# Tile 0 of x loaded first, and three token tiles scaled on ScalarE, in the start-up of a Hedgehog linear-attention and MLP kernel

## The chip, the cores and the metric

The kernel runs on one core of a Trainium2 chip. Time is device time in microseconds (us), and smaller is better. Three runs of the kernel before took 687.21, 686.83 and 685.87 us, with a median of 686.83 us.

## The reference

With x of shape (2048, 640), 32 heads of 20 columns and a hidden width of 1536, the kernel must compute this:

```python
xn = layernorm(x)                               # per token, over 640 columns, eps 1e-5
q, k, v = split(xn @ wqkv)                      # 32 heads x 20
pq, pk = q @ w_phi[h], k @ w_phi[h]             # per head
phi_q = concat(softmax(pq), softmax(-pq))
phi_k = concat(softmax(pk), softmax(-pk))
kv, z = sum_s phi_k^T v, sum_s phi_k            # per head, over all 2048 tokens
s = (phi_q @ kv / (phi_q @ z + 1e-6)) @ wo
g = silu(gelu(xn @ w1 + b1) @ w2 + b2)
out = x + s * g
```

All arithmetic is float32. The kernel gets float32 precision out of TensorE's fp32r format by splitting each operand in a high part (a rounded copy) and a low part (the rest), and by adding three of the four cross products.

## The kernel before, in words

The 2048 tokens are 16 tiles of 128. Phase 1, which is where the change lies, first makes the folded key weights: for each of five chunks of 128 input rows, six TensorE products multiply a chunk of `wqk` (transposed, 384 KB per chunk) with a block diagonal of `w_phi` (`bd`, 360 KB), so that `xn @ wk` gives `pk` at once. `fold` (line 163) issues those products; `fold_w` copies the result out of PSUM as a high part on ScalarE (line 172) and a low part on VectorE (line 173). The folds of the query weights come later, spread over the loop.

A token tile goes through these steps. `x_in` (line 131) loads 128 rows of x. `stats` (lines 186 to 189) takes mean and variance on VectorE, adds eps there, and raises to the power -0.5 on GpSimd. `norm` (line 197) then subtracts the mean and multiplies by the reciprocal deviation over the whole tile, in place, on VectorE. `transpose_x` (line 292) transposes the tile on TensorE in five pieces; `plain` copies it out as a high part on ScalarE (line 226) and a low part on VectorE (line 228). For an odd tile this is in two pieces, `b` and `xp`. `project` (line 306) multiplies the tile with weights in 30 products. A projection has room in its middle, after three of its five chunks, for the transposes of the next tile.

`feat1` (lines 319 to 327) turns `pk` into exponents: maximum, minimum, difference on VectorE, and the negated half on GpSimd. `feat2` (line 332) is the exponential on ScalarE. The value weights `wv` are split in `split_w`: the high part on ScalarE (line 136), the low part on VectorE for chunks 0, 2 and 4 and on GpSimd for chunks 1 and 3 (both line 138). `value` (lines 349 to 354) is the projection with `wv`, and `kv_acc` (line 377) adds a tile's keys and values up. After phase 1 come the MLP and the output, on which TensorE works almost without a pause.

The order of the start-up is written by hand: `phase1` and `startup` are stretches in which each engine issues its instructions in the order of the program text, and an instruction that waits holds everything behind it on its engine. So the lines below are the queue of each engine, as far as each has a part in them. TensorE first runs eleven products of a matrix of ones with itself, whose result nobody reads (line 439).

PSUM has three double banks (`bankA`) for folds, transposes and projections. A step that takes a bank waits until the readers of the bank's last content are done. All loads of this stretch are issued by SyncE, on one queue, in the order of the text; a `stats` tile `st` has two buffers.

Of the kernel before, what the change touches and what calls it, by code (L numbers as in the profile page):

```python
# [8 lines left out]
F32 = mybir.dt.float32  # L9
F32R = mybir.dt.float32r  # L10
AF = mybir.ActivationFunctionType
OP = mybir.AluOpType
# [3 lines left out]
P = 128  # L16
# [29 lines left out]
def hedgehog_gated_mlp_kernel(ctx: ExitStack, tc: tile.TileContext, x, xt_in, wqk, bd, wv, wo, w1, b1, w2, b2, out_t):  # L46
    nc = tc.nc
# [3 lines left out]
    small = ctx.enter_context(tc.tile_pool(name="small", bufs=2))  # L51
# [25 lines left out]
    def slab(dt, name, shape=(P, 2, D)):  # L77
        return slabs.tile(list(shape), dt, tag="S", name=name)
# [4 lines left out]
    def bankA():  # L83
        return pools["A"].tile([P, 2, 512], F32, tag="A", name="pA")

    def bankB(name="pB"):
        return pools["B"].tile([P, 512], F32, tag="B", name=name)
# [41 lines left out]
    def load_x(t):  # L129
        xt = row([P, D], F32, "xt")  # L130
        nc.sync.dma_start(xt[:], x[_tok(t) * P:(_tok(t) + 1) * P, :])
        return xt
# [17 lines left out]
    def load_fold(which, mid=None):  # L150
        tl = folds[:, which]
        for c in range(KC):
            nc.sync.dma_start(tl[:, c], wqk[which, c, :, :6 * P].rearrange("p (i t) -> p i t", i=6))
            if c == 0 and mid is not None:
                mid()
        return tl

    def fold(tl, c):
        ps = bankA()
        for i in range(6):  # L160
            hf, j = divmod(i, 3)
            n = 120 if j < 2 else 80
            mm = nc.tensor.matmul(ps[:, hf, 120 * j:120 * j + n], tl[:n, c, i, :], foldb[:n, i, :n],  # L163
                                  start=True, stop=True)
        return ps, mm

    def fold_w(tl, cs, name, dst):
        for c in cs:
            ps, mm = fold(tl, c)
            sl = slab(F32R, f"{name}{c}")  # L170
            s3 = sl[:].rearrange("p s (a b) -> p s a b", a=2)
            nc.scalar.activation(s3[:, 0], ps[:, :, :HALF], AF.Copy)
            lo = nc.vector.tensor_tensor(s3[:, 1], ps[:, :, :HALF], s3[:, 0].bitcast(F32), op=OP.subtract)
            dst.append(sl)
        return mm, lo
# [5 lines left out]
    def stats(t, sm, mean, rstd):  # L181
        xt = xts.pop(t)
        st = sm[:, :12]
        for i in range(2):
            with tc.issue_after(last_feat[0].ins) if last_feat[0] is not None and not by_hand[0] else ExitStack():
                nc.vector.bn_stats(st[:, 6 * i:6 * i + 6], xt[:, i * HALF:(i + 1) * HALF])
        nc.vector.bn_aggr(sm[:, 12:14], st.rearrange("p (a b) -> p a b", a=2))
        nc.vector.tensor_scalar(rstd, sm[:, 13:14], LN_EPS, None, op0=OP.add)
        nc.gpsimd.tensor_tensor(rstd, rstd, mhalf[:], op=OP.pow)
        if mean is not None:  # L190
            nc.vector.tensor_copy(mean, sm[:, 12:13])
        return xt

    def norm(t):
        sm = small.tile([P, 16], F32, tag="st", name="st")
        xt = stats(t, sm, None, sm[:, 14:15])
        nc.vector.tensor_scalar(xt[:], xt[:], sm[:, 12:13], sm[:, 14:15], op0=OP.subtract, op1=OP.mult)
        xns[t] = xt

    W2 = 2 * P  # L200
# [85 lines left out]
    def transpose_x(t):  # L286
        q, o = divmod(t, 2)
        xn = xns.pop(t)
        ps = bankA()
        flat = ps[:].rearrange("p a b -> p (a b)")  # L290
        for k in range(KC):
            nc.tensor.transpose(flat[:, k * P:(k + 1) * P], xn[:, k * P:(k + 1) * P], ident[:])  # L292
        plain(q, o, flat[:, :D].rearrange("p (k t) -> p k t", t=P))
# [3 lines left out]
    def project(t, ws, mid=None):  # L297
        q, o = divmod(t, 2)
        ps = bankA()
        n = 0  # L300
        for k in range(KC):
            if k == 3 and mid is not None:
                mid()
            for a, b in PASSES:
                for hf in range(2):
                    nc.tensor.matmul(ps[:, hf, :HALF], stat_x(q, o, k, a),  # L306
                                     ws[k][:, b, hf * HALF:(hf + 1) * HALF],
                                     start=n == 0, stop=n == 3 * KC - 1)
                n += 1
        return ps  # L310
# [4 lines left out]
    def feat1(ps):  # L315
        p4 = heads(ps)
        mx = small.tile([P, 2, 16], F32, tag="mx", name="mx")
        mn = small.tile([P, 2, 16], F32, tag="mn", name="mn")
        nc.vector.tensor_reduce(mx[:], p4, axis=AX.X, op=OP.max)
        nc.vector.tensor_reduce(mn[:], p4, axis=AX.X, op=OP.min)  # L320
        e = slab(F32, "e")[:]
        e5 = e.rearrange("p a (h s d) -> p a h s d", s=2, d=DH)
        nc.vector.tensor_tensor(e5[:, :, :, 0, :], p4, mx[:, :, :, None].to_broadcast([P, 2, 16, DH]),
                                op=OP.subtract)
        nr = small.tile([P, 2, 16], F32, tag="nr", name="nr")
        last_feat[0] = nc.vector.tensor_tensor(nr[:], mn[:], mx[:], op=OP.subtract)  # L326
        nc.gpsimd.tensor_tensor(e5[:, :, :, 1, :], nr[:, :, :, None].to_broadcast([P, 2, 16, DH]),  # L327
                                e5[:, :, :, 0, :], op=OP.subtract)
        return e.rearrange("p a b -> p (a b)")
# [51 lines left out]
    vs, es, phis, xns, wk_s, wq_s = {}, {}, {}, {}, [], []  # L381
# [47 lines left out]
    def x_in(t):  # L429
        xts[t] = load_x(t)  # L430
# [4 lines left out]
    phase1 = ExitStack()  # L435
    phase1.enter_context(tc.manual_schedule(engines={mybir.EngineType.PE, mybir.EngineType.SP}))
    pw = bankA()
    for i in range(11):
        nc.tensor.matmul(pw[:, 0, :P], ones[:], ones[:], start=True, stop=True)
    startup = ExitStack()  # L440
    startup.enter_context(tc.manual_schedule())
    nc.sync.dma_start(foldb, bd)
    wkT = load_fold(1, lambda: x_in(0))
    x_in(1)
    x_in(2)
    wv_raw = [load_raw(wv[c * P:(c + 1) * P, :]) for c in range(KC)]
# [9 lines left out]
    def split_v(c):  # L456
        wv_s.append(split_w(wv_raw[c][:], "wv", "pool" if c % 2 else "dve"))

    norm(0)
    fold_w(wkT, range(2), "wk", wk_s)  # L460
    transpose_x(0)
    fold_w(wkT, range(2, 3), "wk", wk_s)
    norm(1)
    fold_w(wkT, range(3, KC), "wk", wk_s)
    kvp[0] = bankB("kv")
    pk = project(0, wk_s, lambda: transpose_x(1))
    norm(2)
    split_v(0)
    split_v(1)
    es[0] = feat1(pk)  # L470
# [5 lines left out]
    split_v(3)  # L476
    feat2(es[0])
    split_v(4)
    norm(3)
    es[1] = feat1(pk)  # L480
    vs[0] = value(0)
    phis[0] = key_fin(es.pop(0))
# [73 lines left out]
    t = NT - 1  # L556
# [494 lines left out]
```

## Time and profile before

| what | value |
|---|---|
| median of three runs | 686.83 us (685.87 to 687.21) |
| the profiled execution, its own time | 688.63 us |
| its span, from the first instruction of the program to the end of the last | 686.9 us |
| TensorE busy | 676.7 us (99%) |
| VectorE, GpSimd, ScalarE busy | 455.5, 375.6, 251.3 us |

The profiled execution took 1.73 us more than its span, and 1.80 us more than the median of the runs. Times in the views below count from the start of the span. In a timeline row stand the start, the length from the first to the last instruction of the row, the engine (PE is TensorE, PEld its weight loads, DVE is VectorE, ACT is ScalarE, POOL is GpSimd, SPq is SyncE's queue), the line, the operation, the tiles as output<-inputs, shapes, a count, and in brackets how long the engine stood idle before and what ended that. An fp32 product appears as two MATMUL records, so that the eleven products of ones are 22 and a fold of six products is 12. A row of the table by stretches gives for each engine its busy time and, in brackets, its instructions; then the granted TensorE clock, the share of the DMA engines that was busy, and GB/s.

### The profile page before, as it was taken

To read this page: it belongs to the slowest core of one execution; us is meant where nothing else is said; L and a number is where in the kernel's file an instruction comes from. 1 tells how busy PE (TensorE), PEld (TensorE's weight loads), DVE (VectorE), ACT (ScalarE), POOL (GpSimd) and SP (SyncE) were. 2 spreads that over 40 slices of the span, in tenths; PEclk is the share of its full clock that TensorE was granted. 3 is DMA by queue.
4 is the path that set the end of the run, shared out by engine and by line. 5 is a ranking of instruction groups with operands and counts; after the bars stand their busy time and mean duration, and the time that the engine had idled before them with its cause. 6 is when DMAs were issued, how large, how long until landed. Compare 5 with 4: busy or idle time off the path is not lost.

```text
span 686.9 us, 11941 instructions
## 1 busy us (share of the span) xinstructions
PE 676.7 (99%) x4713; PEld 590.6 (86%) x4713; DVE 455.5 (66%) x730; ACT 251.3 (37%) x398; POOL 375.6 (55%) x336
## 2 busy tenths in 40 slices
PE   8899999999999999999999999999999999999997
PEld 8899999999999998888887888888888887777875
DVE  4788566886876456677978774676977655774232
ACT  3332313323332237244353347633233354425430
POOL 1355244859577355866968853636456640783221
PEclk9999999999999999999999999999999999999999
DMA  9820052734261153329687697376364491886623
GB/s 339 305 88 2 3 150 81 242 79 149 51 216 59 80 171 134 115 70 329 211 301 260 210 421 319 90 266 240 140 206 153 145 396 49 314 295 210 231 93 107
DMA packets 73966, 125.73 MB, mean 183 GB/s; under 512 B 5694, under 2 KB 42558, under 8 KB 73014
## 3 DMA queue, kind: packets, MB, share of 16 engines
q1 hardware_dynamic: 71606, 114.48, 48.9%
q10 hardware_dynamic: 2304, 10.49, 4.2%
q8 instruction: 37, 0.61, 0.4%
q14 instruction: 19, 0.16, 0.1%
HBM read 79.85 MB, written 45.10 MB: 182 GB/s over the span
## 4 chain that ended last, share of the span: by engine, by line
PE 90%; DVE 5%; ACT 1%; issue 1%; DMA 1%; POOL 1%; SPq 0%; DVEq 0%; POOLq 0%; ACTq 0%
PE pA L306 30%; PE pB L645 22%; PE pB L616 18%; PE pB L804 11%; PE pB L746 3%; PE pB L735 2%; PE kv L377 2%; PE pA L163 2%; DVE y L654 2%; DVE xhi L670 1%; DMA xt<-in_x_dram 1%; PE pA L292 1%; PE pB L753 1%; DVE rc L340 0%; PE pB L590 0%
## 5 line engine op out<-in xcount | busy, mean ns | idle before, releaser
L645 PE MATMUL pB<-hs,w2s 128*128 128x512 f32 x720 | 167.1, 390 | 0.0
L645 PEld LDWEIGHTS pB<-hs,w2s 128*128 128x128 f32 x720 | 134.7, 188 | 29.2 <-PE pB L746 0.8
L616 PE MATMUL pB<-xp,w1s 128*128 128x512 f32 x324 | 81.4, 390 | 1.0 <-DVE pB L888 1.0
L616 PE MATMUL pB<-xd,w1s 128*128 128x512 f32 x324 | 79.3, 389 | 0.0
L332 ACT ACTIVATE e<-e 128x1280 f32<-128x1280 f32 x32 | 40.7, 1272 | 91.5 <-POOL e L327 91.0
L804 PE MATMUL pB<-oT,wo 128*128 128x512 f32 x300 | 72.9, 394 | 0.0
L616 PEld LDWEIGHTS pB<-xp,w1s 128*128 128x128 f32 x324 | 60.7, 188 | 13.9 <-DVE pB L888 1.4
L654 DVE TENSOR_TENSOR y<-pB,y 128x512 f32<-128x512 f32 x100 | 63.9, 680 | 12.3 <-PE pB L645 12.1
L616 PEld LDWEIGHTS pB<-xd,w1s 128*128 128x128 f32 x324 | 60.8, 188 | 12.6
L804 PEld LDWEIGHTS pB<-oT,wo 128*128 128x128 f32 x300 | 55.4, 188 | 14.8 <-ACT ph L738 1.2
L345 POOL TENSOR_TENSOR e<-e,rc 128x1280 f32<-128x1280 f32 x16 | 39.0, 2440 | 48.5 <-DVE rc L365 48.2
L345 POOL TENSOR_TENSOR eq<-eq,rc 128x1280 f32<-128x1280 f32 x16 | 38.0, 2372 | 50.0 <-DVE rc L704 50.0
L327 POOL TENSOR_TENSOR e<-nr,e 128x640 f32<-128x640 f32 x32 | 45.4, 1421 | 33.5 <-DVE nr L326 30.7
L306 PE MATMUL pA<-wv,xp 128*128 128x320 f32 x384 | 61.0, 312 | 0.8 <-DVE nr L326 0.4
L621 ACT ACTIVATE pB<-pB,b1t 128x512 f32<-128x512 f32 x48 | 31.8, 662 | 77.3 <-DVE pB L888 28.4
L306 PE MATMUL pA<-wk,xp 128*128 128x320 f32 x384 | 59.9, 311 | 0.0
L306 PE MATMUL pA<-wq,xp 128*128 128x320 f32 x384 | 59.0, 309 | 0.0
L306 PEld LDWEIGHTS pA<-wv,xp 128*128 128x128 f32 x384 | 56.9, 188 | 1.7 <-issue 0.7
L306 PEld LDWEIGHTS pA<-wq,xp 128*128 128x128 f32 x384 | 56.9, 188 | 0.1
L306 PEld LDWEIGHTS pA<-wk,xp 128*128 128x128 f32 x384 | 56.8, 188 | 0.1
L691 POOL TENSOR_TENSOR ez<-eq,zrep 128x1280 f32<-128x1280 f32 x16 | 47.3, 2953 | 1.1 <-PE pB L753 1.1
L401 POOL TENSOR_TENSOR w1s<-raw,w1s 128x640 fp32r<-128x640 f32 (+1 forms) x18 | 25.7, 1429 | 36.8 <-ACT w1s L400 29.6
(139 smaller groups left out, 1046.0 us busy)
## 6 DMA issues: line engine op xcount, KB each, us to landing
raw<-in_w_dram SPq DMA_DIRECT2D x42, 320.0 KB, 4.4
e_dram<-e ACTq DMA_DIRECT2D x16, 640.0 KB, 3.3
eq<-e_dram SPq DMA_DIRECT2D x16, 640.0 KB, 6.9
phi_dram<-eq SPq DMA_DIRECT2D x16, 640.0 KB, 3.4
phi<-phi_dram SPq DMA_DIRECT2D x16, 640.0 KB, 9.5
xt<-in_x_dram SPq DMA_DIRECT2D x16, 320.0 KB, 4.8
xres<-in_xt_dram SPq DMA_DIRECT2D x20, 256.0 KB, 4.5
out_dram<-xres SPq DMA_DIRECT2D x18, 256.0 KB, 3.0
```

The costliest lines, as they stand in the source:

```text
L306: nc.tensor.matmul(ps[:, hf, :HALF], stat_x(q, o, k, a), ws[k][:, b, hf * HALF:(hf + 1) * HALF], start=n == 0, stop=n == 3 * KC - 1)
L327: nc.gpsimd.tensor_tensor(e5[:, :, :, 1, :], nr[:, :, :, None].to_broadcast([P, 2, 16, DH]), e5[:, :, :, 0, :], op=OP.subtract)
L332: nc.scalar.activation(ef, ef, AF.Exp)
L345: nc.gpsimd.tensor_tensor(e3, e3, rc[:, :, None].to_broadcast([P, 64, DH]), op=OP.mult)
L401: nc.gpsimd.tensor_tensor(sl[:, 1, :n], src, sl[:, 0, :n].bitcast(F32), op=OP.subtract)
L616: nc.tensor.matmul(bank[ch][:], tl[:, a, off + wo_:off + wo_ + P], mov(blk, b), start=new and n == 0, stop=n == len(mms) - 1, skip_group_c ...
L621: nc.scalar.activation(ps, ps, AF.Gelu_apprx_tanh, bias=b1t[:, f:f + 1])
L645: nc.tensor.matmul(ps[:], ws[i][:, b, d * P:(d + 1) * P], hs[o][i][:, a, :], start=i == n == 0, stop=(i, n) == (GF - 1, 2), skip_group_che ...
L654: nc.vector.tensor_tensor(y, ps[:], y, op=OP.add)
L691: nc.gpsimd.tensor_tensor(zv, ef, zf, op=OP.mult)
L746: nc.tensor.matmul(po[64 * e:64 * e + 64, :256], bdk[:n, 2 * j + e, :], ph[:n, e * 256:(e + 1) * 256], start=True, stop=True)
L804: nc.tensor.matmul(ps[:], w, o, start=n == 0, stop=n == 15)
```

## The change

Three things are changed, all in the start-up. The load of tile 0 of x is issued ahead of `bd` and of the first chunk of `wqk`, where it stood third. TensorE runs fourteen products of ones instead of eleven. For tiles 1, 2 and 3, `norm` is replaced by two steps: `norm_stats` takes the statistics as before and then forms minus mean times reciprocal deviation, a 128x1 instruction on VectorE, and `norm_apply` computes x times scale plus bias over the tile on ScalarE. The statistics of tile 2 stand ahead of the first projection, where `norm(2)` stood behind it. Tile 0 and tiles 4 to 15 are treated as before.

```diff
+    def norm_stats(t):
+        sm = small.tile([P, 16], F32, tag="st", name="st")
+        xt = stats(t, sm, None, sm[:, 14:15])
+        nc.vector.tensor_scalar(sm[:, 15:16], sm[:, 12:13], sm[:, 14:15], -1.0, op0=OP.mult, op1=OP.mult)
+        nb[t] = xt, sm
+
+    def norm_apply(t):
+        xt, sm = nb.pop(t)
+        nc.scalar.activation(xt[:], xt[:], AF.Identity, bias=sm[:, 15:16], scale=sm[:, 14:15])
+        xns[t] = xt
...
-    for i in range(11):
+    for i in range(14):
         nc.tensor.matmul(pw[:, 0, :P], ones[:], ones[:], start=True, stop=True)
...
+    x_in(0)
     nc.sync.dma_start(foldb, bd)
-    wkT = load_fold(1, lambda: x_in(0))
+    wkT = load_fold(1)
     x_in(1)
     x_in(2)
...
     fold_w(wkT, range(2, 3), "wk", wk_s)
-    norm(1)
+    norm_stats(1)
     fold_w(wkT, range(3, KC), "wk", wk_s)
+    norm_apply(1)
+    norm_stats(2)
     kvp[0] = bankB("kv")
     pk = project(0, wk_s, lambda: transpose_x(1))
-    norm(2)
+    norm_apply(2)
     split_v(0)
     split_v(1)
     es[0] = feat1(pk)
...
     split_v(4)
-    norm(3)
+    norm_stats(3)
+    norm_apply(3)
     es[1] = feat1(pk)
     vs[0] = value(0)
```

The new lines move the numbering: what is line 172 and 173 stays, line 226 and 228 become 239 and 241, line 306 becomes 319, and so on by 13 (further down by up to 17). The order of each engine shows what the text does to the queues. VectorE, from the sum of tile 1's statistics to the low part of the transposed tile 1 (`b_272` or `b_283`, and `xp`), before:

```order
L187 BN_AGGR st<-st 128x2
L188 TENSOR_SCALAR st<-st 128x1
L197 TENSOR_SCALAR xt<-xt,st 128x640
L173 TENSOR_TENSOR wk_233<-pA,wk_233 128x640
L173 TENSOR_TENSOR wk_243<-pA,wk_243 128x640
L228 TENSOR_TENSOR b_272<-pA,b_272 128x2x128
L228 TENSOR_TENSOR xp<-pA,xp 128x3x128
L186 BN_STATS st<-xt 128x6 x2
L187 BN_AGGR st<-st 128x2
L188 TENSOR_SCALAR st<-st 128x1
L197 TENSOR_SCALAR xt<-xt,st 128x640
```

and the same place in the change:

```order
L187 BN_AGGR st<-st 128x2
L188 TENSOR_SCALAR st<-st 128x1
L205 TENSOR_SCALAR st<-st 128x1
L173 TENSOR_TENSOR wk_236<-pA,wk_236 128x640
L173 TENSOR_TENSOR wk_246<-pA,wk_246 128x640
L186 BN_STATS st<-xt 128x6 x2
L187 BN_AGGR st<-st 128x2
L188 TENSOR_SCALAR st<-st 128x1
L205 TENSOR_SCALAR st<-st 128x1
L241 TENSOR_TENSOR b_283<-pA,b_283 128x2x128
L241 TENSOR_TENSOR xp<-pA,xp 128x3x128
```

The two instructions over the whole tile (line 197) are gone from VectorE, two of one column (line 205) have come, and tile 2's statistics stand ahead of tile 1's low part instead of behind it.

ScalarE, from the high part of the last key weights to the first value copy `v`, in the change:

```order
L172 ACTIVATE wk_246<-pA 128x640
L210 ACTIVATE xt<-xt,st 128x640
L239 ACTIVATE b_283<-pA 128x2x128
L239 ACTIVATE xp<-pA 128x3x128
L210 ACTIVATE xt<-xt,st 128x640
L136 ACTIVATE wv<-raw 128x640 x3
L239 ACTIVATE xp<-pA 128x5x128
L136 ACTIVATE wv<-raw 128x640
L345 ACTIVATE e<-e 128x1280
L136 ACTIVATE wv<-raw 128x640
L210 ACTIVATE xt<-xt,st 128x640
L367 ACTIVATE v<-pA 128x32x20
```

Without its three rows of line 210 this is the order before. The row for tile 1 stands ahead of the high part of transposed tile 1 (`b_283`, `xp`), the one for tile 2 ahead of the five splits of `wv`, and the one for tile 3 behind them and ahead of `v`.

SyncE's first loads, in the change:

```order
L131 DMA xt<-in_x_dram 128x640
L456 DMA folds<-in_bd_dram 128x720
L153 DMA folds<-in_wqk_dram 128x768 x5
L131 DMA xt<-in_x_dram 128x640 x2
L144 DMA raw<-in_wv_dram 128x640 x5
```

Before, `bd` stood first, one load of `wqk` second, tile 0 of x third, and four loads of `wqk` behind it.

More of the change, by code (lines that the diff above doesn't have):

```diff
@@ L197, in norm @@
         nc.vector.tensor_scalar(xt[:], xt[:], sm[:, 12:13], sm[:, 14:15], op0=OP.subtract, op1=OP.mult)
+        xns[t] = xt
+    nb = {}
+    def norm_stats(t):
[6 more added lines that the diff above has]
+        nc.scalar.activation(xt[:], xt[:], AF.Identity, bias=sm[:, 15:16], scale=sm[:, 14:15])
         xns[t] = xt
```

## The prediction

> **What bounds the kernel now.** I read the busy shares first, then the table by stretches, then the timeline of the start. TensorE is the bound, and its idle time lies in the first 35 us:
>
> ```profile
> PE 676.7 (99%) x4713; PEld 590.6 (86%) x4713; DVE 455.5 (66%) x730; ACT 251.3 (37%) x398; POOL 375.6 (55%) x336
> ...
> 6.20:7.70 1.50, 1.46 (x13) 1.31 (x11) 0.07 (x1) 0.00 (x1) 0.00 (x0) 1.00 1.03 389
> ...
> 8.70:10.40 1.70, 1.53 (x13) 1.41 (x13) 0.98 (x4) 0.14 (x1) 0.56 (x1) 1.00 1.02 406
> ...
> 20.00:24.20 4.20, 2.94 (x21) 2.70 (x20) 3.40 (x7) 1.19 (x2) 2.07 (x2) 1.00 0.95 370
> ...
> 26.60:35.00 8.40, 7.61 (x49) 7.06 (x49) 5.24 (x12) 2.60 (x3) 3.87 (x3) 1.00 0.94 279
> 35.00:80.00 45.00, 45.00 (x552) 43.99 (x551) 35.92 (x66) 12.32 (x17) 21.52 (x25) 1.00 0.11 32
> 80.00:680.00 600.00, 599.02 (x3952) 516.00 (x3951) 397.43 (x624) 226.93 (x364) 344.85 (x284) 1.00 0.55 188
> ```
>
> From 35 to 80 us TensorE has no gap, and from 80 to 680 us it has 0.98 us. So what it gains before 35 us reaches the end, as long as the engines that feed it move ahead too. Behind 8.70 us the gaps are 0.17 (8.70 to 10.40), 1.26 (20 to 24.2) and 0.79 us (26.6 to 35): 2.22 us in all. The timeline names them:
>
> ```profile
> 1.20 5.07 PE L439 MATMUL pA<-ones 128*128 128x128 f32 x22 [1.20 <-POOL ones L102]
> 6.06 1.60 PE L163 MATMUL pA<-folds 120*128 120x120 f32 x12
> 8.66 1.56 PE L163 MATMUL pA<-folds 120*128 120x120 f32 x12 [0.99 <-DMA folds<-in_wqk_dram]
> 10.39 0.74 PE L292 MATMUL pA<-ident,xt 128*128 128x128 f32 x5 [0.17 <-DVE xt L197]
> 20.10 1.92 PE L306 MATMUL pA<-wk,b 128*128 128x320 f32 x12
> 24.16 0.74 PE L292 MATMUL pA<-ident,xt 128*128 128x128 f32 x5 [1.26 <-DVE xt L197]
> 27.09 3.17 PE L306 MATMUL pA<-wv,xp 128*128 128x320 f32 x20 [0.44 <-DVE nr L326]
> 30.50 2.11 PE L306 MATMUL pA<-wv,xp 128*128 128x320 f32 x10 [0.24 <-POOL wv L138]
> 35.09 0.71 PE L292 MATMUL pA<-ident,xt 128*128 128x128 f32 x5
> ```
>
> The first fold has its data when the products of ones end. The second waits 0.99 us for its chunk. The transposes of tile 0 wait 0.17 us and those of tile 2 1.26 us for the scaled tile, and the first value projection waits for its bank and then for `wv`.
>
> **Scaling and statistics.** What delays tile 2, and all that stands behind it on VectorE, is this:
>
> ```profile
> 16.62 1.55 DVE L173 TENSOR_TENSOR wk<-pA,wk 128x640 fp32r<-128x640 f32 x2
> 19.68 0.55 DVE L228 TENSOR_TENSOR xp<-pA,xp 128x384 fp32r<-128x384 f32 x1
> 20.14 0.88 DVE L186 BATCH_NORM_STATS2 st<-xt 128x6 f32<-128x320 f32 x2
> 21.30 0.16 DVE L188 TENSOR_SCALAR st<-st 128x1 f32<-128x1 f32 x1
> 22.19 1.83 DVE L197 TENSOR_SCALAR xt<-xt,st 128x640 f32<-128x640 f32 x1 [0.73 <-POOL st L189]
> 23.94 0.81 DVE L138 TENSOR_TENSOR wv<-raw,wv 128x640 fp32r<-128x640 f32 x1
> 26.87 0.18 DVE L326 TENSOR_TENSOR nr<-mn,mx 128x32 f32<-128x32 f32 x1
> 30.88 0.82 DVE L138 TENSOR_TENSOR wv<-raw,wv 128x640 fp32r<-128x640 f32 x1 [2.37 <-ACT wv L136]
> 33.66 0.61 DVE L197 TENSOR_SCALAR xt<-xt,st 128x640 f32<-128x640 f32 x1 [0.73 <-POOL st L189]
> ...
> 22.12 1.55 POOL L138 TENSOR_TENSOR wv<-raw,wv 128x640 fp32r<-128x640 f32 x1
> 27.13 1.79 POOL L327 TENSOR_TENSOR e<-nr,e 128x640 f32<-128x640 f32 x1 [3.46 <-DVE nr L326]
> ...
> 19.19 2.00 ACT L136 ACTIVATE wv<-raw 128x640 fp32r<-128x640 f32 x3
> 30.13 0.72 ACT L136 ACTIVATE wv<-raw 128x640 fp32r<-128x640 f32 x1
> 32.71 0.71 ACT L354 ACTIVATE v<-pA 128x640 f32<-128x640 f32 x1 [1.86 <-PE pA L306]
> ```
>
> Scaling a tile cost VectorE 0.61 us twice and 1.83 us for tile 2, where it ends with GpSimd's `wv` (22.12 + 1.55 = 23.67). The Trainium skill (SBUF — State Buffer, "Who interferes with whom") has a lock for this: such a VectorE instruction and GpSimd's share a port pair, and the second waits for the first. The trace agrees (23.67 plus a part of 0.61 is 24.02); by that rule ScalarE never waits so, and the sum stays the same with or without it.
>
> No row shows the new ScalarE scaling. The nearest, a 128x640 copy, took 0.72 us from SBUF; with a column as bias it may be longer, so I bound it by 0.71 (the copy out of PSUM in the last row) and twice that, and take 0.72 as it reads and writes just as much. The new 128x1 step is like L188, 0.15 us, which is also its lower bound; 0.61, the whole tile, is its upper.
>
> The new times, if TensorE ran as before: VectorE has the last low part of the key weights at about 17.7 instead of 18.17 (0.46 less scaling). Tile 2's statistics follow at once. From their start to the reciprocal deviation it took 22.15 - 20.14 = 2.0 us; with the new step, 19.9. ScalarE is through with tile 1's copies when it begins on `wv`, at 19.2, so tile 2 is scaled at 20.65 instead of 24.02. TensorE wants it at 24.16 - 1.26 = 22.9: **the 1.26 us go**, with 2.2 us to spare. The price is paid by tile 1's low part, which slips from 20.23 to about 20.9; its first half is out at 20.3 and TensorE, which starts on tile 1 at 20.10 with four products of the high part (0.16 us each), wants it at 20.7, so that is covered, by 0.4 us. (Were the step 0.61, half of that is gone.)
>
> ScalarE's splits of `wv` start at 20.65 instead of 19.19. VectorE's first one thus ends near 22.2 instead of 24.75, and `feat1` of tile 0, 2.3 us in the trace (24.75 to 27.05), near 24.5: **the bank wait of 0.44 us goes**. GpSimd's `e` (1.79) ends near 26.4 and its second `wv` (1.55 like the first) near 28.0. TensorE, rid of its gaps, reaches that chunk's low part at 30.50 - 0.24 - 1.70 = 28.6. From the end of `e` to that of the last low part, over the exponential and two splits, the rows give 31.70 - 28.92 = 2.8 us, so it is there near 29.2, when TensorE needs it near 29.7 (2.05 us before 31.7). So **the last 0.35 us go** as well, by margins of 0.5 us.
>
> New waits: line 210 for tile 3 stands ahead of `v`, whose bank the transposes of tile 3 take. From the end of the last `wv` low part (31.70) to the reciprocal deviation was 33.66 - 31.70 = 1.96 us; so the new step ends at 31.3, the scaling at 32.0 and `v` (0.71) at 32.75. TensorE was there at 35.09 and will be at 35.09 - 2.05 = 33.0: covered, by 0.3 us. `feat1` of tile 1 starts behind the new step instead of behind 0.61 us of scaling, near 31.3 instead of 34.27, so the keys of later tiles lead more than TensorE does.
>
> Sum behind the transposes of tile 0: 1.26 + 0.44 + 0.35 = **2.05 us saved**.
>
> **Order of loads and products of ones.** The first loads, in the order of the queue, and how long each took from issue to landing (for the second, third, fourth and sixth place):
>
> ```profile
> 1.25 0.42 SPq L153 DMA_DIRECT2D folds<-in_wqk_dram  x1
> 1.72 0.42 SPq L131 DMA_DIRECT2D xt<-in_x_dram  x1
> 2.19 1.85 SPq L153 DMA_DIRECT2D folds<-in_wqk_dram  x4
> ...
> folds<-in_wqk_dram SPq DMA_DIRECT2D x1, 384.0 KB, 3.4
> xt<-in_x_dram SPq DMA_DIRECT2D x1, 320.0 KB, 5.9
> folds<-in_wqk_dram SPq DMA_DIRECT2D x1, 384.0 KB, 6.4
> folds<-in_wqk_dram SPq DMA_DIRECT2D x1, 384.0 KB, 7.3
> ...
> 7.63 0.89 DVE L186 BATCH_NORM_STATS2 st<-xt 128x6 f32<-128x320 f32 x2 [5.78 <-DMA xt<-in_x_dram]
> 9.63 0.61 DVE L197 TENSOR_SCALAR xt<-xt,st 128x640 f32<-128x640 f32 x1 [0.68 <-POOL st L189]
> ```
>
> So the second, third and fourth place landed near 4.65, 7.6 and 8.6. Tile 0 goes from third place to first: landing to scaled is 10.24 - 7.6 = 2.6 us, so it is ready before 7.3 even if it lands like the second place. That removes the 0.17 us. But the first chunk of `wqk` goes from second to third, and through the third place the same 1,064 KB have to come. From the row it lands at 7.6, where the first fold started at 6.06. From the other side: if it comes as early as the second place did plus its own 384 KB at 389 GB/s (1.0 us), it is there at 5.7. I take 7.6, the same place in the queue. The fourth place does not change.
>
> The three products of ones are six records more: at the pace of the first 22 (4.86/22 = 0.221 us) 1.33 us, at that of the folds (1.60/12 = 0.133) 0.80 us. They end at 6.9 to 7.4, inside the wait for the chunk; without that cover they would cost their full 0.80 to 1.33 us.
>
> So the folds run 7.63 to 9.23 and on to 10.79, their 1.60 and 1.56 us back to back, and the transposes start at 10.79 instead of 10.39: **0.40 us lost**.
>
> **Sum.** -2.05 + 0.40 = -1.65 us, against the profiled execution's own 688.63: 686.98. The median of the runs shown is 1.80 us lower, so 686.83 - 1.65 = **685.2 us**.
>
> **Rivals.**
>
> - *The chunk lands early (5.7).* The folds then wait only for the fourth place at 8.6, end at 10.22, and tile 0 is ready: all 2.22 us are saved, 684.6. For it: the third place took 2.5 us more than the second for 320 KB more, which are 0.8 us at 389 GB/s; such a delay need not recur. Against it: the transfers moved 389 GB/s up to 7.7 us, so the queue was full.
> - *A new wait on ScalarE.* `v` and the last splits now stand behind scalings that wait for statistics, with margins of 0.3 to 0.5 us. If the scaling takes 1.4 us instead of 0.72, once ahead of the splits and once ahead of `v`, `v` ends at 32.75 + 1.36 = 34.1, the transposes of tile 3 start 1.1 us later and 0.55 us is left: 686.3. The same side has executions in which early loads come fast: there tile 0 was no wait before either, and the added products cost their 0.80 us: 2.05 - 0.80 = 1.25, 685.6.
> - *TensorE falls back to the slower pace (slower than before).* Its first 22 records ran at 0.221 us and the folds at 0.133, so TensorE has a slower pace, and products of ones lead out of it. If the chunk comes at 9.0 (7.3 us after issue, as long as the slowest `wqk` load took), TensorE stands idle some 2 us ahead of its folds, more than the 0.99 us that did no harm. The transposes then start at 12.2, 1.8 us late; if the slower pace returns for 4.86 us, 22 records lose 0.09 us each, 1.9 us. 1.8 + 1.9 - 2.05 = +1.65: 688.5. It is beyond 0.2% from a landing near 8.7 on, and only with the slower pace; the late landing alone ends at -0.25.
>
> *A page beside the last rival.* By the Trainium skill (TensorE: Matmul & The Clock Gate, "What's actually happening") the clock opens after a busy window of about 3.4 us and closes after an idle one of that length, free-running. The 4.86 us at the slower pace agree with it; by it 2 us of idleness would close nothing and the last rival would be -0.25 us, and more products of ones would open the clock no sooner.
>
> **How the numbers follow.** Chances: forecast 0.45 (its own range 684.8 to 685.8, as the chunk and the margins move it by a few tenths), early chunk 0.22, new wait or nothing to gain from loads 0.26, slower pace 0.07. A measurement of this kernel tells a change of 0.2%, 1.37 us, from none, so faster is below 685.46. The forecast is there in two of three cases (0.31), the early chunk always (0.22), the third hardly (0.03): 0.56 faster. Same has the rest of the forecast, of the third and a part of the last: 0.39. Slower: 0.05. The range goes from 684.1, all gaps closed and half a microsecond of the spread of the runs, to 686.8, the new wait with the same.
>
> **What would show it.** Right: the first chunk's fold starts behind a DMA wait near 7.6; tile 2's transposes, the first value projection and its `wv` have no idle time ahead of them; no transposes of tile 3 wait for ScalarE; TensorE is full from about 9 us on. Wrong: a wait of TensorE for line 210 or for `v`, fold records above 0.133 us, or gaps behind 35 us that give the lead back.

## The result and the profile after

The changed kernel took 684.45 us in the median of seven runs (683.99 to 686.25). Seven runs of the kernel before, the three shown among them, have a median of 686.70. The ratio is 0.9972, with a 95% interval from 0.9960 to 0.9983: 1.9 us saved (1.2 to 2.7), where 1.65 were forecast. The two medians lie 2.25 us apart, inside that interval.

The profiled execution took 684.19 us with a span of 682.4. That is 4.4 us less than the one of before, and more than the change is worth, as the second trace of each kernel shows further down.

The stretches of the changed kernel that answer to those shown of before (TensorE's busy time and records come first, GB/s last):

```profile
20.00:24.20 4.20, 4.20 (x32) 4.19 (x31) 3.60 (x6) 3.15 (x5) 1.97 (x2) 1.00 1.04 405
26.60:35.00 8.40, 8.06 (x54) 7.29 (x53) 6.44 (x12) 3.20 (x5) 2.51 (x6) 1.00 0.68 207
35.00:80.00 45.00, 45.00 (x553) 44.00 (x551) 33.86 (x65) 12.17 (x19) 20.75 (x25) 1.00 0.11 31
80.00:680.00 600.00, 597.63 (x3939) 514.52 (x3937) 397.44 (x622) 226.33 (x362) 345.47 (x281) 1.00 0.55 188
```

The 1.26 us between 20 and 24.2 us are gone. (In the last row TensorE's last product ends inside the stretch; up to there the trace shows no wait of TensorE behind 35 us.) The timeline of TensorE in the changed kernel, and then of its weight loads:

```profile
1.20 5.93 PE L452 MATMUL pA<-ones 128*128 128x128 f32 x28 [1.20 <-POOL ones L102]
6.96 2.80 PE L163 MATMUL pA<-folds 120*128 120x120 f32 x24
9.60 0.71 PE L305 MATMUL pA<-ident,xt 128*128 128x128 f32 x5
21.79 0.71 PE L305 MATMUL pA<-ident,xt 128*128 128x128 f32 x5
24.10 5.19 PE L319 MATMUL pA<-wv,xp 128*128 128x320 f32 x30
32.15 0.77 PE L305 MATMUL pA<-ident,xt 128*128 128x128 f32 x5 [0.22 <-ACT v L367]
...
27.18 0.88 PEld L319 LDWEIGHTS pA<-wv,xp 128*128 128x128 f32 x6 [0.25 <-POOL wv L138]
28.43 0.59 PEld L319 LDWEIGHTS pA<-wv,xp 128*128 128x128 f32 x4 [0.37 <-DVE wv L138]
32.15 0.53 PEld L305 LDWEIGHTS pA<-ident,xt 128*128 128x128 f32 x5 [0.48 <-ACT v L367]
```

The folds follow the products of ones without a wait, as their first chunk had landed 4.5 us after its issue at 1.73 us, and the transposes of tile 0 and tile 2 (rows at 9.60 and 21.79) have none either. The value projection at 24.10 starts at once, but inside it the weight loads wait 0.25 us for GpSimd's and 0.37 us for VectorE's low part of `wv`. The transposes of tile 3 wait for `v`, which they did not before.

VectorE, GpSimd's splits of `wv` and ScalarE in the changed kernel:

```profile
18.77 0.21 DVE L205 TENSOR_SCALAR st<-st 128x1 f32<-128x1 f32 x1 [0.73 <-POOL st L189]
20.60 0.83 DVE L138 TENSOR_TENSOR wv<-raw,wv 128x640 fp32r<-128x640 f32 x1 [0.82 <-ACT wv L136]
23.54 0.18 DVE L339 TENSOR_TENSOR nr<-mn,mx 128x32 f32<-128x32 f32 x1
27.55 0.82 DVE L138 TENSOR_TENSOR wv<-raw,wv 128x640 fp32r<-128x640 f32 x1 [2.36 <-ACT wv L136]
...
21.27 1.57 POOL L138 TENSOR_TENSOR wv<-raw,wv 128x640 fp32r<-128x640 f32 x1 [2.54 <-ACT wv L136]
25.55 1.58 POOL L138 TENSOR_TENSOR wv<-raw,wv 128x640 fp32r<-128x640 f32 x1
...
19.02 0.92 ACT L210 ACTIVATE xt<-xt,st 128x640 f32<-128x640 f32 x1 [0.67 <-DVE st L205]
19.84 1.98 ACT L136 ACTIVATE wv<-raw 128x640 fp32r<-128x640 f32 x3
30.58 0.93 ACT L210 ACTIVATE xt<-xt,st 128x640 f32<-128x640 f32 x1 [3.06 <-DVE st L205]
31.41 0.68 ACT L367 ACTIVATE v<-pA 128x640 f32<-128x640 f32 x1
```

ScalarE scales a tile in 0.92 us; tile 2 is ready at 19.94, where TensorE wants it at 21.79. The last two rows show the new wait: `v` had to stand behind the scaling of tile 3.

### The profile page after: what moved, and what is told of

Same layout as the page of the kernel before. It is cut to its first block, busy times and chain, and to the rows that moved or that the text cites. A ratio compares the mean times of both kernels' runs of the same rounds, so it can differ in the third digit from the quotient of the medians.

```text
span 682.4 us, 11960 instructions
## 1 busy us (share of the span) xinstructions
PE 676.1 (99%) x4719; PEld 591.2 (87%) x4719; DVE 452.7 (66%) x730; ACT 253.9 (37%) x401; POOL 376.9 (55%) x336
## 4 chain that ended last, share of the span: by engine, by line
PE 96%; DVE 1%; POOL 1%; ACT 1%; issue 1%; POOLq 0%; DVEq 0%
PE pA L319 29%; PE pB L662 24%; PE pB L633 22%; PE pB L821 11%; PE pB L763 3%; PE pB L752 2%; PE kv L390 2%; PE pA L163 2%; PE pA L452 1%; PE pA L305 1%; PE pB L770 1%; DVE st L186 0%; DVE wk L173 0%; PE pB L607 0%; ACT wv L136 0%
```

## The experiments

Eleven kernels were run, and of three of them a second execution was profiled. The chips differ, so the ratio compares each kernel with runs of the kernel before on the same chip, whose medians were 686.46 to 686.70 us. From the traces two numbers were read (starts of rows of the timeline, in us): when the transposes of tile 0 start, which is what loads and products of ones decide, and how long it is from there to the transposes of tile 3, which is what scaling and statistics decide, as long as TensorE runs at its full pace.

| kernel | loads | products of ones | tile 0 | tile 0 to tile 3 | median us | ratio (95%) |
|---|---|---|---|---|---|---|
| before, first trace | old | 11 | 10.39 | 24.70 | 686.70 | |
| before, second trace | old | 11 | 9.48 | 24.70 | | |
| load order alone | new | 11 | 10.06 | 24.53 | 686.88 | 1.0006 (0.9996 to 1.0016) |
| scaling and statistics alone | old | 11 | 9.17 | 22.51 | 684.61 | 0.9970 (0.9960 to 0.9980) |
| the change, first trace | new | 14 | 9.60 | 22.55 | 684.45 | 0.9972 (0.9960 to 0.9983) |
| the change, second trace | new | 14 | 10.09 | 22.56 | | |
| with 11 products | new | 11 | 12.47 | 23.29 | 685.14 | 0.9985 (0.9972 to 0.9998) |
| the same, second trace | new | 11 | 9.56 | 22.53 | | |
| with 6 products | new | 6 | 11.92 | 23.30 | 688.77 | 1.0030 (1.0020 to 1.0041) |
| `v` first | new | 14 | 9.49 | 22.15 | 684.64 | 0.9969 (0.9958 to 0.9980) |
| statistics of tile 2 late | new | 14 | 10.30 | 25.01 | 687.32 | 1.0007 (0.9999 to 1.0015) |
| scaled on VectorE | new | 14 | 9.21 | 23.63 | 686.43 | 0.9997 (0.9989 to 1.0005) |
| `wv` on VectorE | old | 11 | 9.46 | 21.53 | 683.38 | 0.9952 (0.9939 to 0.9965) |
| the same, new loads | new | 14 | 10.68 | 21.53 | 684.10 | 0.9962 (0.9948 to 0.9975) |

### The load order alone

```diff
+    x_in(0)
     nc.sync.dma_start(foldb, bd)
-    wkT = load_fold(1, lambda: x_in(0))
+    wkT = load_fold(1)
```

> The load order alone: tile 0 of x first, eleven products of ones, scaling and statistics as before. Theory (order and scaling are two separate gains): the transposes of tile 0 start near 9.6 us as in the changed kernel, 0.8 us sooner than in the trace of before, all later waits of before stay as they are (1.26 us ahead of the transposes of tile 2, about 0.8 us at the first value projection), so 0.4 to 0.8 us are saved: near 686.1. Rival (the early landing of the first chunk in the one trace was luck; the third place lands near 7.6 again): the transposes start near 10.8, 0.4 us are lost: near 687.1.

686.88 us, ratio 1.0006: nothing gained. TensorE now waits ahead of the first fold instead of the second:

```profile
1.20 4.50 PE L439 MATMUL pA<-ones 128*128 128x128 f32 x22 [1.20 <-POOL ones L102]
7.16 3.07 PE L163 MATMUL pA<-folds 120*128 120x120 f32 x24 [1.45 <-DMA folds<-in_wqk_dram]
10.06 0.71 PE L292 MATMUL pA<-ident,xt 128*128 128x128 f32 x5
23.66 0.73 PE L292 MATMUL pA<-ident,xt 128*128 128x128 f32 x5 [1.25 <-DVE xt L197]
```

The theory's 0.4 to 0.8 us are refuted; the rival's 687.1 is inside the interval. The later waits (1.25 us here) are those of before, as both had it.

### Scaling and statistics alone

The change with the load order and the eleven products of before.

```diff
-    x_in(0)
     nc.sync.dma_start(foldb, bd)
-    wkT = load_fold(1)
+    wkT = load_fold(1, lambda: x_in(0))
...
-    for i in range(14):
+    for i in range(11):
```

> Scaling on ScalarE and the earlier statistics alone: bd and the first chunk of wqk ahead of tile 0, eleven products of ones. Theory: the start up to the transposes of tile 0 is that of before, and behind it 1.26 us ahead of the transposes of tile 2, the bank wait of 0.44 us and part of the 0.35 us are gone: 1.8 to 2.1 us saved, near 684.7. Rival (the lead of the changed kernel comes from the loads): under 1 us saved, above 685.7, with a wait left ahead of the transposes of tile 2.

684.61 us, 0.9970: the whole gain of the change, as the theory had it. Loads and products of ones add nothing that can be measured.

### The change with eleven and with six products of ones

```diff
-    for i in range(14):
+    for i in range(11):
```

> The whole change with eleven products of ones instead of fourteen. Theory (the three products only fill the wait for the first chunk): the first fold starts when its chunk lands, near 6.3 us instead of 6.96, the second still waits for its own chunk near 7.7, so the transposes of tile 0 start 0 to 0.3 us sooner and the time is that of the changed kernel within 0.3 us: 684.1 to 684.5. Rival (without them TensorE falls back to its slower pace): fold records of 0.22 us instead of 0.13, 1 to 2 us lost, 685.5 or more.

685.14 us, and its twelve runs are spread from 684.15 to 688.42. The profiled one is the longest of them:

```profile
1.20 5.06 PE L452 MATMUL pA<-ones 128*128 128x128 f32 x22 [1.20 <-POOL ones L102]
7.30 5.38 PE L163 MATMUL pA<-folds 120*128 120x120 f32 x24 [1.04 <-DMA folds<-in_wqk_dram]
12.47 1.27 PE L305 MATMUL pA<-ident,xt 128*128 128x128 f32 x5
13.54 4.39 PE L163 MATMUL pA<-folds 120*128 120x120 f32 x36
```

Behind a wait of 1.04 us the 24 fold records took 5.38 us, 0.22 us each, where the change had 2.80. The median lies between the theory (684.1 to 684.5) and the rival (685.5 or more), but this execution has the rival's slow records. A longer wait did no harm with the load order alone (1.45 us), so a second execution was profiled.

> The whole change with eleven products of ones, looked at once more. Theory (the wait for the first chunk decides by chance whether TensorE keeps its slower pace): if the wait is 0.5 us or less, folds at 0.13 us a record and about 684.4; if it is 1 us as in the first trace, folds at 0.22 us until about 14 us and 686 to 688.4. Rival (the pace has nothing to do with the wait): the one without the other.

The one run took 685.24 us and shows this:

```profile
1.20 4.24 PE L452 MATMUL pA<-ones 128*128 128x128 f32 x22 [1.20 <-POOL ones L102]
6.74 2.99 PE L163 MATMUL pA<-folds 120*128 120x120 f32 x24 [1.29 <-DMA folds<-in_wqk_dram]
```

A longer wait, 1.29 us, and folds at full pace: the theory as written falls, since it had the length of the wait decide. What differs is the row ahead. Here the 22 records of ones took 4.24 us, so TensorE had come to its full pace before the wait; in the first trace they took 5.06, 0.23 each to the end, so it had not.

With six products this is forced, as they end long before that point:

```diff
-    for i in range(14):
+    for i in range(6):
```

> The whole change with six products of ones: they end near 3.9 us, and TensorE stands idle until the first chunk lands, 2.5 to 3.3 us. Theory (an idle stretch ahead of the folds keeps TensorE at its slower pace, as in the one trace with eleven products): fold records near 0.22 us in the folds of the first chunks, the transposes of tile 0 start near 12 us, 2 to 4 us lost against the changed kernel, 686.5 to 688.5. Rival (the slower pace of that trace was chance, the idle stretch costs nothing): 684.2 to 685.

```profile
1.20 2.93 PE L452 MATMUL pA<-ones 128*128 128x128 f32 x12 [1.20 <-POOL ones L102]
6.75 5.38 PE L163 MATMUL pA<-folds 120*128 120x120 f32 x24 [2.62 <-DMA folds<-in_wqk_dram]
```

688.77 us, 4.3 us more than with fourteen by the medians (4.0 by the ratios, as the chips differ), and all eight runs above 687.6. The theory of an idle stretch that keeps the slower pace holds, in this form: the stretch does harm when it comes before the pace has changed. The median lies above its upper expectation of 688.5, which is still inside the interval.

### Tile 3 scaled behind `v`

```diff
     norm_stats(3)
-    norm_apply(3)
     es[1] = feat1(pk)
     vs[0] = value(0)
+    norm_apply(3)
```

> The whole change, with tile 3 scaled behind the first value copy v instead of ahead of it. Theory (the 0.22 us that the transposes of tile 3 waited for v come from the scaling that stood ahead of it): v ends near 29.9 us, the transposes of tile 3 start without a wait, 0.2 us saved against the changed kernel, near 684.2. Rival: the wait only moves to the scaling itself, which then ends as late, or to the bank of the next projection, and the time does not change: 684.45.

```profile
31.64 0.71 PE L305 MATMUL pA<-ident,xt 128*128 128x128 f32 x5
```

The transposes of tile 3 start without a wait, at 31.64, and 22.15 us behind tile 0's instead of 22.55. The wait was real and came from the order on ScalarE. The median, 684.64, cannot show the 0.4 us: the interval of this comparison is 1.5 us wide.

### Late statistics, and scaling on VectorE

```diff
     norm_apply(1)
-    norm_stats(2)
...
+    norm_stats(2)
     norm_apply(2)
```

> The whole change, but the statistics of tile 2 stay where they were, behind the low part of tile 1 on VectorE; scaling stays on ScalarE. Theory (both the earlier statistics and the scaling off VectorE are needed): the reciprocal deviation of tile 2 comes 2.0 us after the low part of tile 1, the scaling 1.1 us later, so the transposes of tile 2 wait some 0.4 us; the wait of 1.83 us of VectorE's scaling beside GpSimd is gone. 1.4 to 1.8 us saved, near 684.9. Rival (the earlier statistics are the whole gain): 0.7 us or less saved, above 685.7.

687.32 us: nothing is left of the gain. The theory's 684.9 is refuted; the time lies on the rival's side (above 685.7), but whether the early statistics are the whole gain is for the next kernel to tell. A wait on ScalarE of the kind that the prediction named as a rival is there:

```profile
19.42 0.55 DVE L241 TENSOR_TENSOR xp<-pA,xp 128x384 fp32r<-128x384 f32 x1
22.17 0.92 ACT L210 ACTIVATE xt<-xt,st 128x640 f32<-128x640 f32 x1 [3.12 <-DVE st L205]
23.00 1.98 ACT L136 ACTIVATE wv<-raw 128x640 fp32r<-128x640 f32 x3
23.15 0.77 PE L305 MATMUL pA<-ident,xt 128*128 128x128 f32 x5 [0.50 <-ACT xt L210]
23.76 0.83 DVE L138 TENSOR_TENSOR wv<-raw,wv 128x640 fp32r<-128x640 f32 x1 [1.62 <-ACT wv L136]
26.93 1.26 PE L319 MATMUL pA<-wv,xp 128*128 128x320 f32 x7 [1.26 <-DVE nr L339]
```

The transposes of tile 2 wait 0.50 us, as expected (0.4). But ScalarE stands 3.12 us at the scaling with the splits of `wv` queued behind, so VectorE waits 1.62 us for the first of them, and `feat1`, behind it, gives the bank 1.26 us late instead of 0.44.

Then the other half alone: early statistics, with the scaling on VectorE.

```diff
-        nc.scalar.activation(xt[:], xt[:], AF.Identity, bias=sm[:, 15:16], scale=sm[:, 14:15])
+        nc.vector.tensor_scalar(xt[:], xt[:], sm[:, 14:15], sm[:, 15:16], op0=OP.mult, op1=OP.add)
```

> The whole change, but tiles 1 to 3 are scaled on VectorE (one instruction with scale and bias) with the earlier statistics. Theory (the earlier statistics alone let VectorE scale tile 2 before GpSimd begins on wv, so in 0.61 us): no wait ahead of the transposes of tile 2, the same time as the changed kernel within 0.4 us, 684.1 to 684.9. Rival (ScalarE is what matters, VectorE's scaling again meets GpSimd's work and takes 1.8 us): the 1.26 us wait or most of it stays, 685.5 or more.

686.43 us, 0.9997: the theory's 684.1 to 684.9 is refuted. The rival's time (685.5 or more) came, but without its wait, and the theory's mechanism came half true:

```profile
16.31 0.60 DVE L210 TENSOR_SCALAR xt<-xt,st 128x640 f32<-128x640 f32 x1
19.79 0.60 DVE L210 TENSOR_SCALAR xt<-xt,st 128x640 f32<-128x640 f32 x1
20.31 2.19 DVE L138 TENSOR_TENSOR wv<-raw,wv 128x640 fp32r<-128x640 f32 x1
...
19.93 1.90 POOL L138 TENSOR_TENSOR wv<-raw,wv 128x640 fp32r<-128x640 f32 x1 [1.09 <-ACT wv L136]
```

Tile 2 is scaled in 0.60 us and there is no wait ahead of its transposes. But the low part of `wv` behind it now takes 2.19 instead of 0.81 us, and tile 1's scaling (16.31) stands behind the low parts of the key weights. TensorE waits 0.44 us for tile 1 and 0.35 us for the bank. From tile 0 to tile 3 the trace is still 1.07 us shorter than before, of which the runs show 0.2 us (0.3 lost to 0.8 gained). So neither half alone brings the gain of the two together.

### The rest of the waits taken away

Loads and eleven products as before, scaling and statistics as in the change, `v` first, and:

```diff
-        wv_s.append(split_w(wv_raw[c][:], "wv", "pool" if c % 2 else "dve"))
+        wv_s.append(split_w(wv_raw[c][:], "wv", "pool" if c == 1 else "dve"))
...
     split_v(3)
-    feat2(es[0])
     split_v(4)
+    feat2(es[0])
```

> Loads and eleven products of ones as before, scaling and statistics as in the change, and three more edits at the first value projection: tile 3 scaled behind v, the low part of the fourth wv chunk on VectorE instead of GpSimd, the fifth wv chunk split ahead of the first exponential. Theory (what is left there are the waits for the low parts of wv, about 0.6 us, and 0.2 us for v): TensorE goes through the first value projection without a wait, 0.6 to 0.8 us saved against the scaling alone (684.6): near 684.0. Rival (these waits only move to the next exponentials and their scaling on GpSimd): the time stays at 684.6.

```profile
23.95 4.56 PE L319 MATMUL pA<-wv,xp 128*128 128x320 f32 x30
28.35 1.92 PE L319 MATMUL pA<-wv,b 128*128 128x320 f32 x12
30.99 0.71 PE L305 MATMUL pA<-ident,xt 128*128 128x128 f32 x5
```

683.38 us, 0.9952: faster than both kernels in the median, and more than the theory's 0.6 to 0.8 us below the scaling alone, though the intervals of the ratios just overlap (0.9939 to 0.9965 here, 0.9960 to 0.9983 for the change). The rival's 684.6 lies outside. The value projection takes 4.40 us to the next one (23.95 to 28.35) instead of 5.03 in the change (24.10 to 29.13 in its timeline). From tile 0 to tile 3 it is 21.53 us, 1.0 us less than the change, of which `v` first gave 0.4; the two edits of `wv` were not tried apart.

### The same with the new loads, and second traces

The kernel above with `x_in(0)` first and fourteen products:

> The kernel with the low parts of wv on VectorE, and with it the load order and the fourteen products of ones of the change. Theory (order and products of ones cancel: tile 0 was hardly a wait, and the products fill a wait that the order itself makes): the same time as without them, 683.4, within 0.4 us. Rival (the order gains its 0.2 to 0.8 us once the later waits are gone): 682.6 to 683.1.

684.10 us, with the first fold at 7.96 behind a wait of 1.43 us for its chunk. The theory's 683.0 to 683.8 is missed by 0.3 us to the other side; the intervals of the two (0.9939 to 0.9965 and 0.9948 to 0.9975) overlap, and the order gains nothing here either.

> The kernel before, looked at once more. Theory (its one trace lies at the top of its spread: 688.63 us against a median of 686.7): a time near 686.7, the transposes of tile 0 near 9.2 to 9.8 us instead of 10.39, the same waits of 1.26 and about 0.8 us behind them, and less than the 0.98 us of idleness near 372 us. Rival: the start is always as in that trace, and the time differs elsewhere.

687.01 us; tile 0 at 9.48 us, then waits of 1.26, 0.44 and 0.24 us as in the first trace, and 0.38 us of idleness from 80 to 680 us, at another place than the 0.98 us. So the start and the late gap differ by execution, and the distance of 24.70 us does not.

> The changed kernel, looked at once more. Theory: the first chunk lands anywhere from 6.1 to 7.5 us, the transposes of tile 0 start between 9.2 and 10.3, no wait of TensorE but 0.6 us for the low parts of wv and 0.2 us for v: 684 to 685.3. Rival: a wait that the first trace did not have.

685.66 us, above the expected 684 to 685.3; the first fold at 7.38 us behind a wait of 1.05 us for its chunk, tile 0 at 10.09, and once 0.6 us for `phi` late in the program: the rival's wait that the first trace did not have. The rows between tile 0 and tile 3 are those of the first trace.

## Why the prediction was right

The forecast was 685.2 us, in a range of 684.1 to 686.8; it came to 684.45. The direction and the mechanism hold. Inside the sum one step failed and several sizes were off, and their errors nearly cancel, which is luck.

**Scaling and statistics: 2.05 us forecast, 2.15 measured** (24.70 to 22.55 us, in two traces of each), and 2.1 by the ratio of the runs with scaling and statistics alone. The waits of 1.26 us ahead of tile 2's transposes and of 0.44 us for the bank are gone, as put. The starts of the rows shown (first traces) tell what each stretch gave, in us:

| stretch | before | change | saved | forecast |
|---|---|---|---|---|
| transposes of tile 0 to transposes of tile 2 | 13.77 | 12.19 | 1.58 | 1.26 |
| from there to the value projection | 2.93 | 2.31 | 0.62 | 0.44 |
| from there to the transposes of tile 3 | 8.00 | 8.05 | -0.05 | 0.35 |

The first two gave more than the idle time that was counted. (In the first, 0.17 us came at tile 0, for which TensorE had waited before: with the load order alone this stretch is 13.60 us.) The third gave nothing, and here the step failed: "The last 0.35 us go as well, by margins of 0.5 us". Waits of 0.25 and 0.37 us for `wv` stayed, and `v`, which was to be covered by 0.3 us, cost the transposes of tile 3 0.40 us, as the kernel with `v` first shows.

The low parts of `wv` were not late for this. Counted from the transposes of tile 0, the last of GpSimd and the last of VectorE were forecast to end after 17.6 and 18.8 us, and they ended after 17.5 and 18.8 (rows at 25.55 and 27.55). But TensorE, put at 18.2 and 19.3 us, wanted them for its weight loads at 17.3 and 18.5. `v` ended after 22.5 us instead of 22.4, with the scaling at 0.92 us and not 0.72, while TensorE, put at 22.6, would have been there at 22.15. So what was wrong is the time at which TensorE comes for its data: it had been worked out by taking off the idle time of the products alone, which shows only part of the waits. Its weight loads show more, in the trace of before:

```profile
24.13 0.53 PEld L292 LDWEIGHTS pA<-ident,xt 128*128 128x128 f32 x5 [1.50 <-issue]
27.06 2.94 PEld L306 LDWEIGHTS pA<-wv,xp 128*128 128x128 f32 x20 [0.67 <-issue]
30.50 0.88 PEld L306 LDWEIGHTS pA<-wv,xp 128*128 128x128 f32 x6 [0.50 <-POOL wv L138]
31.76 0.59 PEld L306 LDWEIGHTS pA<-wv,xp 128*128 128x128 f32 x4 [0.38 <-DVE wv L138]
```

(`issue` stands where the profile shows nothing that was waited for. The products of these two rows wait for `xt` and `nr`.) These are 3.05 us, where the idle of the products was put at 2.05; and the kernel that takes all of them away is 3.17 us shorter from tile 0 to tile 3. Less the 1.10 us that the weight loads still wait in the change (0.25, 0.37 and 0.48) they give 1.95, and with the 0.17 us at tile 0 2.12, against 2.15 measured.

**Loads and products of ones: 0.40 us lost was forecast.** The single pair of traces says the opposite, 0.79 us gained (10.39 to 9.60), which is the rival of the early chunk: it landed 4.5 us after its issue instead of 5.9. But all traces together say that this was the draw of an execution. With the old loads tile 0's transposes start at 10.39, 9.48, 9.17 and 9.46, 9.63 in the mean; with the new ones and fourteen products at 9.60, 10.09, 9.49, 10.30, 9.21 and 10.68, 9.90 in the mean. That is 0.27 us later, with a spread of over 1 us in each; neither these few traces nor the medians tell it from zero. The step "the same place in the queue" was sound: from issue to landing the third place took 4.4 to 5.9 us with tile 0 in it (four traces) and 4.4 to 6.1 with the first chunk of `wqk` (ten traces). Its size was read from the one trace of before, where it took 5.9 us, which lies near the far end.

**The rival on ScalarE** is there in the change, as the wait for `v`. It is larger in the kernel with late statistics: 687.3, past the 686.3 that was worked out for it, because not a longer scaling but a later start of it holds `wv` back. So one of the prediction's signs of being wrong came, a wait of TensorE for `v`. The second trace of the change also has a gap of 0.6 us behind 35 us. Neither gave the gain back.

**The rival of the slower pace** is not in the change, but one step from it. Its price was put at 1.9 us for a return over 4.86 us; six products of ones cost 4.3 us in the median, and from the first fold to the transposes of tile 3 their trace has 28.47 us (6.75 to 35.22) where the change has 25.19 (6.96 to 32.15), 3.3 us more. The fourteen products cost little. In three of their six traces the folds still waited behind them for their chunk (1.05, 1.43 and 1.61 us). In the other three they did not wait, and there the products can have held the folds up: in the first trace the chunk had landed near 6.2 us, and the folds began at 6.96. No run separates that. In return they keep TensorE busy past the point where the pace changes: with eleven the median is 685.14 against 684.45, which the intervals do not separate, and single runs go up to 688.42.

**The sum** by what was measured: -2.15 + 0.27 = -1.88 us, against -1.9 by the ratio. As the 0.27 us are not told from zero, this agreement is no test of them. Both second traces are needed for the sum: the first trace of before lay 1.9 us above its median, with a gap of 0.98 us near 372 us that the second does not have. What ends up in that gap was not tried.

## What to carry to other kernels

When an instruction moves to a queue that works in order, look at what it will wait for and at what is queued behind: the same scaling on ScalarE was worth 2 us with its statistics early, and nothing with them late. Such a move also brings TensorE sooner to everything behind it, so a margin there has to be counted against that earlier time. Read TensorE's waits from the weight loads, not from the idle of the products alone. Take a start-up from several executions before a term of the sum is read from it, and time a reordering of loads that only moves a wait from one chunk to another as a change of its own: here it gained nothing that could be measured.

## What the runs showed of the hardware

**TensorE keeps its slower pace longer when its stream of products is broken early.** Over seven traces, 22 records of ones took from 4.15 to 5.07 us, so the pace changes at a different point in each execution. An idle stretch of 1.04 us that came before this point put it off to near 14 us, some 13 us after the first product: the 36 fold records from 13.54 us on took 4.39 us, against 4.17 in the change. One of 2.62 us, with six products, did the same. Stretches of 1.05 to 1.61 us ahead of the folds that came after it, in five traces, did nothing: there the 24 fold records took 2.88 to 3.07 us. In the trace with eleven products, the table by stretches counts it:

```profile
7.30:12.50 5.20, 5.20 (x25) 5.20 (x26) 0.82 (x1) 0.70 (x1) 0.00 (x0) 1.00 1.03 407
14.00:20.00 6.00, 6.00 (x50) 6.00 (x50) 4.34 (x10) 3.52 (x5) 0.55 (x1) 1.00 1.04 413
```

25 records in 5.20 us are 0.21 us each, where the change has its fold records at 2.80/24 = 0.12. The granted clock is given as 1.00 in both rows, so here the pace has to be read from the counts. The rule that the prediction named (the Trainium skill, TensorE: Matmul & The Clock Gate, "What's actually happening") has the clock open after a busy window of about 3.4 us of a free-running count. That agrees with a point that moves by execution. The prediction drew from it that an idle stretch of 2 us would close nothing; for an open clock no run here speaks against it (the longest such stretch was 1.61 us), but before the opening 1.04 us was enough to put it off.

**A stall between VectorE and GpSimd moved with the order.** The 1.83 us of VectorE's scaling beside GpSimd's `wv` vanished from the scaling in the kernel that scales early on VectorE, and came back as 2.19 us in the next instruction that reads two operands, the low part of `wv`. The lock that the prediction named from the Trainium skill (SBUF — State Buffer, "Who interferes with whom") covers both: scaling, and an instruction with two inputs in SBUF, against GpSimd's reads. In that kernel's trace GpSimd's `wv` ends at 21.83 us and VectorE's low part 0.67 us later, which agrees.

**ScalarE's scaling with a column of scale and one of bias** took 0.92 us for 128x640, 0.20 us more than its copy of the same size from SBUF (0.72).
